# Moving a softmax-row reload one layer earlier in a fused four-layer decode forward and backward, with its zero stores dealt differently

## Chip, cores and metric

The kernel runs on one core of one Trainium2 chip. The metric is the device time of one execution in microseconds (us); lower is better. A core has a matrix engine (PE, with its weight loads shown apart as PEld), a vector engine (DVE), a scalar engine (ACT), GpSimd (POOL) and SyncE (SP), which here only issues transfers; 16 DMA engines carry out the transfers.

## What is computed

One token goes through four layers (attention A, MLP B, A, B, all with shared weights), each with a layer norm and a residual, and then the gradients of all eight inputs are taken for a given `grad_out`. Cut to what matters:

```python
def A(x, k_cache, v_cache, wq, wo):        # 32 heads, 4 key groups, window of the last 4096 keys
    q = (x @ wq) by heads;  k, v = last 4096 rows of the caches
    p = softmax(q k^T / sqrt(128));  return (p v) @ wo
def B(x, w1, b1, w2):
    h = x @ w1 + b1
    return (h * tanh(softplus(h))) @ w2
x = A_x
x = x + A(layernorm(x)); x = x + B(layernorm(x))
x = x + A(layernorm(x)); x = x + B(layernorm(x))
# outputs: x and d/d(A_x, k_cache, v_cache, wq, wo, w1, b1, w2) of <x, grad_out>
```

D is 1024, F 3584, and the caches hold 4 groups x 32768 keys x 128 in bfloat16. Only the last 4096 keys of each group get a gradient. The other 28672 rows of both cache gradients are zeros, and have to be written: 112 stores of 512 KB, 58.7 MB of the 98.8 MB that the kernel writes.

## The kernel before

The layers are called A1, B2, A3, B4; the forward goes through them in this order and the backward comes back. All weights that fit stay in SBUF: `wq`, `wo`, `K` and `V` are four tiles of 8 MB or 4 MB. w1 and w2 do not fit and are streamed through rings of 512 KB buffers. During the MLPs such a ring lies in `K`'s tile (`rings["rb"]`: six buffers over K's groups 1 to 3 in B2's backward), so that K's groups have to be loaded again for A1's backward. `pump` (L172) issues whatever stands next in one written-down queue of loads as soon as its buffer is released by `rel` (L203). K's groups 1, 2 and 3 are the last three entries of that queue; a group needs two buffers, so a group goes out after every second release in the last steps of B2's backward.

All bulk transfers are issued by SP, in the order of the program. The framework gives them eight semaphores in turn, so a transfer is issued only when the one eight issues before it has landed; one whose buffer is not free yet holds up all behind it.

The zero stores are the filler. `zeros(n)` (L139) issues the next n of the 112 from a zeroed source: `zlo` (1024 wide, read twice), `zt` (2048), or, in the last stage, `z8` (4096, which can take two stores in one transfer of 1 MB if they are neighbours and the first has an even number). Where they are issued is written by hand: lists of counts per step (`[8, 4, 17]` in A3's forward, `ZB4` behind the four blocks of B4, `[5, 1, 5]` in A3's backward, L838 in B2's backward, `zeros(4)` and step 0's `zeros(8)` in A1's backward, and a count per output job).

`misc` is a tile of 3072 columns in three parts: `sB` (0 to 1023), `sA` (1024 to 2047) and `zlo`. A1's forward leaves its softmax rows (128 x 1024 bfloat16, 256 KB) in `sA`, and GpSimd stores them to `p1_d` in DRAM (L544), because `sA` then serves as a weight buffer. A3's forward leaves its rows in `sB`. In a layer's backward (`attn_bwd`, L742) the steps are: a product of the gradient with `wo` into two banks (`big`), column sums of it (`acc`), the scores against V (again `big`), a row sum into `sd` (L773), then L776, which forms the score gradient `ds_t` from `big`, `sd` and the softmax rows `p_t`; then `to_keys` transposes it (L436, into `kp`), `keys_mm` multiplies it with K into `R`, and `dqpair` and a product with `wq` follow. In A1's backward (`last`), `p_t` is `wo[:, 0, :]`, free once the first product has read `wo`: GpSimd loads `p1_d` into it (L751), then runs `wo_dead` (L1023: memsets and copies that spread the rows for the output products, which use `wo`'s space as well).

The output stage writes the weight gradients as outer products. Its jobs begin inside A1's backward, from step 3 on (`out_step`): seven pairs for w2 (two halves each), sixteen for w1 interleaved with sixteen for V's and K's gradients (`kv_step`, which takes the softmax rows of A3 and A1 from `p_l` and their score gradients from `ds_l`), then wo and wq. Every job is products on PE, evictions on DVE and ACT into one of seven staging buffers, and a store.

Of the kernel before, what the change touches and what calls it, by code (L numbers as in the profile page):

```python
# [9 lines left out]
BF16 = mybir.dt.bfloat16  # L10
# [4 lines left out]
P = 128  # L15
# [6 lines left out]
def kernel(  # L22
# [22 lines left out]
    nc = tc.nc  # L45
# [15 lines left out]
    WC = W // NC  # L61
# [4 lines left out]
    dram = ctx.enter_context(tc.tile_pool(name="dram", bufs=1, space=bass.MemoryType.DRAM))  # L66
# [17 lines left out]
    wo = kt([P, HQ, D], BF16, "wo")  # L84
# [14 lines left out]
    k_v = A_k_cache[0, :, Sk - W:, :].rearrange("g (p t) d -> p g t d", p=P)  # L99
    v_v = A_v_cache[0, :, Sk - W:, :].rearrange("g (p t) d -> p g t d", p=P)  # L100
    p1_d = dram.tile([P, WC], BF16, name="p1_d")


    x_row, g_row, b_row = kpf[0:TD, 0:P], kpf[0:TD, P:2 * P], kpf[0:NW2, 2 * P:4 * P]
# [34 lines left out]
    def zeros(n, after=None):  # L139
        while n > 0 and zero_jobs:  # L140
            zf, i = zero_jobs.pop(0)
            k = 1
            if zsrc[1] == 4096 and n > 1 and zero_jobs and zero_jobs[0][1] == i + 1 and i % 2 == 0:
                zero_jobs.pop(0)
                k = 2
            dst = zf[:, i * 2048:(i + k) * 2048]
            if zsrc[1] == 1024:
                d = nc.sync.dma_start(dst.rearrange("p (a b) -> p a b", a=2), zlo[:, None, :].to_broadcast([P, 2, 1024]))
            else:
                d = nc.sync.dma_start(dst, zsrc[0][:, 0:k * 2048])  # L150
            gate(d, after)
            after = None
            n -= k
# [588 lines left out]
    def attn_bwd(g_col, g_bf, l, sv, last, nxt, F_, Z_, step):  # L742
        fill_kind("wo")
        big = two_banks()
        for d in range(TD):
            for n in range(8):
                mm(big[n // 4][32 * (n % 4):32 * (n % 4) + 32, :].rearrange("p (h x) -> p h x", h=4),
                   bc(g_bf[:, d:d + 1]), wo[:, 4 * n:4 * n + 4, d * P:(d + 1) * P], d == 0, d == TD - 1, tile_position=(0, 32 * (n % 4)))
        if last:
            p_t, ds_t = wo[:, 0, :], wo[:, 1, :]  # L750
            nc.gpsimd.dma_start(p_t, p1_d[:])  # L751
            wo_dead()
        else:
            p_t, ds_t = sv["p"], sA
        zeros(Z_[0])
        acc = one_tile("acc", HQ)
        j_cols(big, acc, 8, F_[0], True)
        do32 = wk("do32", HQ)
        nc.vector.tensor_copy(pad[:, :, 0:8], acc[:].rearrange("p (g h) -> p g h", g=G))
        nc.vector.tensor_copy(do32[:], acc[:])  # L760
        pr = jkf[:, 0:P]
        nc.vector.tensor_mul(pr[:].rearrange("p (c h) -> p c h", c=NC), do32[:, None, :].to_broadcast([P, NC, HQ]),
                             sv["o32"][:, None, :].to_broadcast([P, NC, HQ]))
        nc.gpsimd.tensor_copy(dos[:, LI[l], :], do32[:])
        step(0)
        fill(F_[1])
        fill_kind("V")
        big = two_banks()
        scores(big, Vf, False)
        sps = sm_tile(P, 1)  # L770
        mm(sps[:], pr[:], one[:], True, True)
        sd = wk("sd", 1)
        nc.vector.tensor_copy(sd[:], sps[:])  # L773
        zeros(Z_[1])
        for h in range(2):
            nc.vector.scalar_tensor_tensor(out=ds_t[:, h * 512:(h + 1) * 512], in0=big[h][:], scalar=sd[:, 0:1],  # L776
                                           in1=p_t[:, h * 512:(h + 1) * 512], op0=ALU.subtract, op1=ALU.mult)
        sv["p"], sv["ds"] = p_t, ds_t
        step(1)
        fill(F_[2])  # L780
        to_keys(ds_t)
        fill_kind("K")
        qacc = one_tile("acc", HQ)
        step(2)
        keys_mm(K[:], fold, qacc, F_[3])
        if not last:
            rings["rb"] += range(2, 8)
            pump()
        nc.scalar.activation(dqpair[:, LI[l], :], qacc[:], ACT.Copy, scale=scale)
        zeros(Z_[2])  # L790
        step(3)
        fill_kind("wq")
        R = one_tile("R", 512)
        for h in range(HQ):
            for hf in range(2):
                g = 2 * hf + h % 2
                mm(R[32 * g:32 * g + 32, :].rearrange("p (t d) -> p t d", t=4), bc(dqpair[:, LI[l], h:h + 1]),
                   wq[:, 4 * hf:4 * hf + 4, h * P:(h + 1) * P], h < 2, h >= HQ - 2, tile_position=(0, 32 * g))
            if h % 4 == 3 and h < 31:
                step(4)  # L800
        y = d_cols(R, hook=lambda: step(5))
        tt = wk("xx", 2 * TD)
        nc.vector.tensor_copy(tt[:, 0:TD], y[:])
        return ln_bwd(tt, sv, g_col, nxt, hook=lambda: step(6))

    def mlp_B2_bwd(g_col, g_bf, sv, x3):
        bcast_g(g_bf)
        R, dps, ds = w2_pass(apair[:, 0, :], g_bf, {10: 1})
        zeros(3)
        dh = kt([P, TF], FP32, "dh_B2")  # L810
        da_merge(dh[:], dps, ds, sv["dact"][:])
        nc.vector.tensor_copy(hpair[:, 1, :], dh[:])
        y = d_cols(R)
        x4_bf = kt([P, TD], BF16, "x4_bf")
        nc.vector.tensor_add(x4_bf[:], x3[:], y[:])

        NT, NV = 4, 3
        dhb = [kpf, jk[:]]
        for hf in range(2):
            for v in range(2):  # L820
                ncb = 2 if v == 0 else 1
                ps = ptile(FP32, "dhp")
                for i in range(ncb):
                    for tt in range(2):
                        col = hf * NW2 + 2 * (NT + 2 * v + i) + tt
                        mm(ps[:, i * 256 + tt:i * 256 + tt + 255:2], bc(hpair[:, 1, col:col + 1], P), ident_bf[:], i == 0 and tt == 0, True)
                evac(dhb[hf][:, v * 512:v * 512 + ncb * 256], ps[:, 0:ncb * 256], ncb * 256, "DA"[(hf + v) % 2])
        nacc = one_tile("acc", TD)
        nv = wk("nv", 16)
        pend = []  # L830

        def pairs(i, w, ring, sl):
            t, hf = i // 2, i % 2
            for k in range(8):
                fb = hf * NW2 + k
                mm(nacc[:, t:t + 1], w[:, k * P:(k + 1) * P], hpair[:, 1, fb:fb + 1], i == 0 and k == 0, hf == 1 and k == 7)
            rel(ring, sl)
            zeros(i in (11, 12, 13, 14))  # L838

        for i in range(16):  # L840
            w, ring, sl = take(("w1h", i))
            T8([w[:, (k // 2) * 256 + k % 2:(k // 2) * 256 + k % 2 + 255:2] for k in range(8)], w[:, 0:1024], "A")
            ttr(w[:, 1024:1792], dhb[i % 2][:, 0:768], nv[:, i:i + 1])
            if pend:
                pairs(*pend.pop())
            pend.append((i, w, ring, sl))
        pairs(*pend.pop())
        tt = wk("xx", 2 * TD)
        n3 = nv[:].rearrange("p (t h) -> p t h", h=2)
        t3 = wk("t3", TD)  # L850
        nc.vector.tensor_add(t3[:], n3[:, :, 0], n3[:, :, 1])
        nc.vector.tensor_add(tt[:, 0:TD], t3[:], nacc[:])
        sv["dh"] = dh
        return ln_bwd(tt, sv, g_col, "A1"), x4_bf
# [133 lines left out]
    def w1_job(t, hf):  # L988
        st = stage()
        wide_job(row_sp["w1"], t, hf, F, st)  # L990
        nc.sync.dma_start(out_6[t * P:(t + 1) * P, hf * (F // 2):(hf + 1) * (F // 2)], st[:, 0:F // 2])
# [27 lines left out]
    w2_out = out_8.rearrange("(c p t) d -> c p t d", p=P, t=2)  # L1019
# [3 lines left out]
    def wo_dead():  # L1023
# [34 lines left out]
        def add(kind, n, f, z=0):  # L1058
            jobs.append((True, f, z))
            while after:  # L1060
                jobs.append((False, after.pop(0), 0))
            for pre, post in prep.get((kind, n), []):
                got = []
                jobs.append((False, lambda pre=pre, got=got: got.append(pre()), 0))
                after.append(lambda post=post, got=got: post(got[0]))

        for n in range(NW2 // 2):
            add("w2a", n, lambda c=2 * n: pair_half(row_sp["w2"], c, w2_out, w2_lhs, 0))
            add("w2", n, lambda c=2 * n: pair_half(row_sp["w2"], c, w2_out, w2_lhs, 1), (0, 0, 1, 1, 0, 0, 1)[n])
        for n in range(16):  # L1070
            add("w1", n, lambda t=n // 2, hf=n % 2: w1_job(t, hf), n in (0, 2, 7))
            add("kv", n, lambda n=n: kv_step(n))
        for n in range(HQ // 8):
            add("wo", n, lambda c=4 * n: tall_jobs(row_sp["wo"], range(c, c + 4), wo_out, wo_lhs))
# [31 lines left out]
        elif i > 2:  # L1106
            run_jobs(1 if i == 4 else 2)

    ZB4 = [10, 10, 10, 8]
    FT4 = [(0, 0, 0, 0), (6, 2, 2, 2), (6, 2, 2, 2), (8, 3)]  # L1110
    FB4 = [(1, 0), (1, 0), (1, 0), (1, 2)]

    pump()
    x1, sA1 = attn_fwd(x0, "A1", True, sA, [0] * 6, [0] * 4)
    x2, sB2, da4 = mlp_B2_fwd(x1)
    x3, sA3 = attn_fwd(x2, "A3", False, sB, [3, 2, 8, 2, 2, 2], [8, 4, 17])
    tt, sB4 = mlp_B4(x3, da4)
    g3, g3b, _ = ln_bwd(tt, sB4, gcol, "A3", nfill=2)
    g2, g2b, _ = attn_bwd(g3, g3b, "A3", sA3, False, "B2", [4, 3, 5, 2], [5, 1, 5], lambda i: None)
# [42 lines left out]
```

## Time and profile before

| | |
|---|---|
| median of three runs | 442.67 us (439.08 to 443.94) |
| profiled execution | 440.81 us, of which its span is 439.0 us |
| bytes moved | 169.45 MB, 386 GB/s over the span |
| busy: PE, DVE, ACT, POOL | 324.2, 234.0, 219.2, 14.7 us |
| SP's transfer queue, share of the 16 engines | 97.9% |
| mean granted TensorE clock | 0.748 |
| store of the softmax rows to DRAM (L544), issue to landing | 6.3 us |
| load of them from DRAM (L751), issue to landing | 8.8 us |
| zero stores from `misc` (98), median issue to landing | 10.7 us |
| loads of a K group (nine), least, median, most | 8.2, 17.7, 20.9 us |

Times in the profile count from the span's start. A group is named by its line, engine, and what it writes from what it reads; a line can be that of a helper (L237 is every product, L257 every transpose of a full tile, L228 and L230 the copies out of PSUM on DVE and ACT, L885 and L888 those of the output stage). In lists of waits the columns are the total, how often, and the longest, in us. A rough map by start of the stage: A1's forward 0, B2's forward 70, A3's forward 114, B4 forward and backward 147, A3's backward 218, B2's backward 249, A1's backward 299, output jobs alone from about 349 on.

### The profile page before, as it was taken

How to read it: one execution, taken by the hardware profiler on the slowest of the kernel's cores; microseconds unless marked ns; L12 is line 12 of the kernel's file. 1: busy time of each engine (PE TensorE's matmuls, PEld its weight loads, DVE VectorE, ACT ScalarE, POOL GpSimd, SP SyncE). 2: the span in 40 equal slices, each digit the busy share in tenths (PEclk: the TensorE clock that was granted, in tenths of full speed). 3: DMA queues.
4: the chain of work that ended last, by engine and by line, in shares of the span. 5: the costliest groups of instructions: out<-in, count | busy, mean ns of one | idle time of the engine just before them, and what ended most of it. 6: DMA issues, size and time to landing. Idle time of an engine off the chain costs nothing.

```text
span 439.0 us, 9214 instructions
## 1 busy us (share of the span) xinstructions
PE 324.2 (74%) x3732; PEld 190.4 (43%) x3732; DVE 234.0 (53%) x532; ACT 219.2 (50%) x335; POOL 14.7 (3%) x52
## 2 busy tenths in 40 slices
PE   3486646378788868778799787897489899999830
PEld 1164215355466656566567465673222322322100
DVE  2035102078345453555546477682146999899950
ACT  1045000047255363555535166682248789899950
POOL 2000000000000000000000000001200020000000
PEclk9998655569699998999999888856765555555555
DMA  8999999999999999899999999999988899999997
GB/s 330 425 421 414 412 408 387 377 368 363 412 411 407 417 403 394 297 385 382 415 403 397 374 408 328 403 329 374 415 345 354 330 392 403 403 406 413 408 414 312
DMA packets 49911, 169.45 MB, mean 386 GB/s; under 512 B 4784, under 2 KB 5836, under 8 KB 45644
## 3 DMA queue, kind: packets, MB, share of 16 engines
q1 hardware_dynamic: 49552, 168.31, 97.9%
q8 instruction: 29, 0.48, 0.4%
q0 software_dynamic: 256, 0.54, 0.3%
q14 instruction: 14, 0.11, 0.1%
q10 hardware_dynamic: 60, 0.01, 0.0%
HBM read 70.00 MB, written 98.84 MB: 385 GB/s over the span
## 4 chain that ended last, share of the span: by engine, by line
PE 22%; DMA 15%; ACT 8%; DVE 4%; issue 2%; ACTq 0%; SPq 0%; DVEq 0%; POOLq 0%
DMA K<-in_B_w_dram 6%; PE R L237 5%; DMA out_dram<-misc 5%; PE tp L257 4%; PE op L237 4%; ACT wo L888 4%; ACT wq L888 3%; PE sm L237 2%; PE acc L237 2%; DMA wo<-p_d 2%; PE lo L237 1%; PE tp L919 1%; DVE wo L885 1%; PE hi L237 1%; DMA out_dram<-wo 1%
## 5 line engine op out<-in xcount | busy, mean ns | idle before, releaser
L230 ACT COPY K<-tp 128x1024 bf16<-128x1024 bf16 x59 | 58.1, 1015 | 17.6 <-PE tp L257 16.5
L257 PE MATMUL tp<-ident_bf,K 128*128 128x128 bf16 x656 | 54.2, 243 | 6.7 <-ACT K L230 3.0
L237 PE MATMUL op<-wo 2*128 2x512 bf16 (+2 forms) x123 | 50.4, 565 | 4.4 <-ACT wo L888 2.2
L257 PEld LDWEIGHTS <-K 128*128 128x128 bf16 x656 | 45.5, 110 | 14.0 <-issue 10.6
L230 ACT COPY wo<-tp 128x1024 bf16<-128x1024 bf16 x33 | 33.5, 1023 | 33.4 <-PE tp L257 30.3
L237 PEld LDWEIGHTS <-wo 128*128 128x128 bf16 (+2 forms) x590 | 23.1, 102 | 55.4 <-issue 45.3
L888 ACT CAST wo<-op 128x512 bf16<-128x512 f32 (+1 forms) x51 | 31.7, 638 | 5.7 <-ACT K L888 1.5
L589 DVE CUSTOM_DVE_ANT_0 K<-K,kp 128x1024 bf16<-128x1024 bf16 (+1 forms) x22 | 24.6, 1127 | 7.2 <-PE R L237 3.8
L228 DVE COPY jk<-R 128x512 f32<-128x512 f32 (+1 forms) x11 | 7.3, 666 | 34.9 <-PE R L237 34.9
L257 PE MATMUL tp<-ident_bf,wo 128*128 128x128 bf16 x336 | 25.7, 231 | 0.3 <-ACT wo L230 0.3
L237 PE MATMUL acc<-wo 2*128 2x512 bf16 (+1 forms) x41 | 24.4, 595 | 0.0
L237 PE MATMUL lo<-wo 2*128 2x512 bf16 x41 | 24.3, 593 | 0.0
L237 PE MATMUL hi<-wo 2*128 2x512 bf16 x41 | 24.3, 592 | 0.0
L257 PEld LDWEIGHTS <-wo 128*128 128x128 bf16 x336 | 20.8, 103 | 7.2 <-issue 7.2
L228 DVE COPY wo<-tp 128x1024 bf16<-128x1024 bf16 x19 | 12.9, 690 | 16.8 <-PE tp L257 16.8
L230 ACT CAST jk<-hi 128x512 bf16<-128x512 f32 x4 | 2.6, 658 | 38.1 <-PE hi L237 38.1
L237 PE MATMUL sm<-wo 2*128 2x512 bf16 (+1 forms) x33 | 20.1, 608 | 0.9 <-DVE cols L377 0.9
L228 DVE COPY K<-tp 128x1024 bf16<-128x1024 bf16 x23 | 15.6, 690 | 9.1 <-PE tp L257 9.0
L885 DVE CAST wo<-op 128x512 bf16<-128x512 f32 (+1 forms) x32 | 18.5, 601 | 3.4 <-PE lo L237 1.7
L228 DVE CAST jk<-lo 128x512 bf16<-128x512 f32 x4 | 2.8, 712 | 32.4 <-PE lo L237 32.4
L237 PE MATMUL R<-wo 2*128 2x512 bf16 (+1 forms) x33 | 19.7, 596 | 0.0
L230 ACT COPY wq<-tp 128x1024 bf16<-128x1024 bf16 x14 | 14.1, 1014 | 11.2 <-PE tp L257 8.4
(293 smaller groups left out, 647.4 us busy)
## 6 DMA issues: line engine op xcount, KB each, us to landing
out_dram<-misc SPq DMA_DIRECT2D x98, 512.0 KB, 10.7
out_dram<-wo SPq DMA_DIRECT2D x36, 512.0 KB, 5.6
K<-in_B_w_dram SPq DMA_DIRECT2D x28, 512.0 KB, 6.8
K<-in_A_k_cache_dram SPq DMA_DIRECT2D x9, 1024.0 KB, 17.7
wq<-in_A_wq_dram SPq DMA_DIRECT2D x8, 1024.0 KB, 10.1
out_dram<-wq SPq DMA_DIRECT2D x8, 1024.0 KB, 11.3
K<-in_B_w_dram SPq DMA_DIRECT2D x16, 448.0 KB, 5.0
out_dram<-wo SPq DMA_DIRECT2D x16, 448.0 KB, 5.8
```

The lines of the kernel that those rows point to most:

```text
L228: return nc.vector.tensor_copy(out_ap, in_ap)
L230: return nc.scalar.copy(out_ap, in_ap)
L237: return nc.tensor.matmul(out_ap, lhsT=lhsT, rhs=rhs, start=start, stop=stop, skip_group_check=True, **kw)
L257: nc.tensor.transpose(ps[:, b * P:(b + 1) * P], ap, ident_bf[:])
L589: return nc.vector.tensor_tensor_reduce(out=w, in0=w, in1=vec, scale=1.0, scalar=0.0, op0=ALU.mult, op1=ALU.add, accum_out=acc_col)
L885: nc.vector.tensor_copy(out_ap, in_ap)
L888: nc.scalar.copy(out_ap, in_ap)
L919: nc.tensor.transpose(ps[:, j * P:(j + 1) * P], spread_t[:, j, :], ident_bf[:])
```

## The change

A1's rows are read back from DRAM in A3's backward, right behind the step that has last read A3's own rows in `sB`: GpSimd first stores A3's rows to a new DRAM buffer `p3_d`, then loads A1's into `sB`. In A1's backward `p_t` is then `sB`, and `wo[:, 0, :]` takes A3's rows from `p3_d`, behind `wo_dead`, for use by V's gradient jobs. In `kv_step` the two layers' rows are thereby found in each other's former place.

The zero stores are counted differently: 14 instead of 17 in A3's last step; 11 instead of 10 behind each of B4's first two blocks; in B2's backward two behind step 9 and one each behind steps 12 and 14, instead of one each behind 11 to 14; one behind each of w2's seven pairs instead of three in all, and none behind w1's jobs instead of three. On SP's queue the end of B2's backward reads, before: K, 2 stores, K, 2 stores, K, 4 stores; after: 2 stores, K, store, K, store, K, 4 stores.

```diff
     p1_d = dram.tile([P, WC], BF16, name="p1_d")
+    p3_d = dram.tile([P, WC], BF16, name="p3_d")
...
         if last:
-            p_t, ds_t = wo[:, 0, :], wo[:, 1, :]
-            nc.gpsimd.dma_start(p_t, p1_d[:])
+            p_t, ds_t = sB, wo[:, 1, :]
             wo_dead()
+            nc.gpsimd.dma_start(wo[:, 0, :], p3_d[:])
         else:
             p_t, ds_t = sv["p"], sA
...
         sv["p"], sv["ds"] = p_t, ds_t
+        if not last:
+            nc.gpsimd.dma_start(p3_d[:], sB)
+            nc.gpsimd.dma_start(sB, p1_d[:])
+            sv["p"] = wo[:, 0, :]
         step(1)
...
             rel(ring, sl)
-            zeros(i in (11, 12, 13, 14))
+            zeros({9: 2, 12: 1, 14: 1}.get(i, 0))
...
-            add("w2", n, lambda c=2 * n: pair_half(row_sp["w2"], c, w2_out, w2_lhs, 1), (0, 0, 1, 1, 0, 0, 1)[n])
+            add("w2", n, lambda c=2 * n: pair_half(row_sp["w2"], c, w2_out, w2_lhs, 1), 1)
         for n in range(16):
-            add("w1", n, lambda t=n // 2, hf=n % 2: w1_job(t, hf), n in (0, 2, 7))
+            add("w1", n, lambda t=n // 2, hf=n % 2: w1_job(t, hf))
...
-    ZB4 = [10, 10, 10, 8]
+    ZB4 = [11, 11, 10, 8]
...
-    x3, sA3 = attn_fwd(x2, "A3", False, sB, [3, 2, 8, 2, 2, 2], [8, 4, 17])
+    x3, sA3 = attn_fwd(x2, "A3", False, sB, [3, 2, 8, 2, 2, 2], [8, 4, 14])
```

## The prediction

> **What bounds the kernel now.** I read the slices first, then the stages, the chain of waits, the timeline around its long wait, and SyncE's own waits. The page's slices show the transfer engines (DMA row) full nearly everywhere and no compute engine full before slice 25. The stages, each asked for by itself, show how full that is in bytes; columns are length, busy us of PE, PEld, DVE, ACT and POOL, granted clock, share of the DMA engines, GB/s:
>
> ```profile
> 292.00:300.00 8.00, 5.67 (x72) 4.62 (x70) 4.78 (x16) 4.53 (x5) 0.00 (x0) 0.50 0.91 285
> 300.00:324.00 24.00, 15.79 (x178) 7.70 (x178) 4.86 (x12) 6.14 (x8) 5.38 (x20) 0.78 1.02 416
> 324.00:352.00 28.00, 25.49 (x169) 7.65 (x168) 22.13 (x48) 21.77 (x41) 0.00 (x0) 0.50 0.82 329
> 352.00:424.00 72.00, 64.81 (x332) 17.54 (x330) 66.90 (x122) 66.92 (x135) 4.42 (x17) 0.50 1.02 405
> 424.00:436.00 12.00, 0.00 (x0) 0.00 (x0) 0.00 (x0) 0.00 (x0) 0.00 (x0) 0.50 1.01 414
> ```
>
> The reader should see two things. After 424 nothing computes and the queue still drains for 12 us, so the end belongs to the transfers: it is the bytes left, at the 405 to 414 GB/s of the last two rows (I use 408), plus whatever holes come before. And there are two holes late in the kernel: 292 to 300 at 285 GB/s lacks (408-285) x 8 = 0.98 MB, or 2.4 us, and 324 to 352 lacks (408-329) x 28 = 2.2 MB, or 5.4 us. Between them lies the wait that the change removes. The chain of waits (start, us, what):
>
> ```profile
> 304.92 0.25 PE lo L237 x4
> 305.18 0.50 issue
> 305.69 8.79 DMA wo<-p_d
> 314.58 1.42 DVE wo L776 x2
> 316.04 0.61 PE tp L436 x4
> 316.65 0.85 PE tp L919 x8
> 317.50 3.39 PE R L237 x27
> ```
>
> In the last attention backward the softmax rows of layer 1 come from DRAM into `wo[:,0,:]`, and L776 waits for them. What else L776 needs was there long before, by the timeline:
>
> ```profile
> 309.00 0.16 DVE L773 COPY cols<-sm 128x1 f32<-128x1 f32 x1 [1.89 <-PE sm L237]
> ...
> 314.58 0.75 DVE L776 SCALAR_TENSOR_TENSOR wo<-lo,cols,wo 128x512 bf16<-128x512 f32 x1 [5.42 <-DMA wo<-p_d]
> ```
>
> That is 5.42 us of pure wait. What is late next is K. Its three head groups reload at 293.0, 295.5 and 299.1, and the product at 317.5 (R from K) reads all of them. No row shows the third one's landing, but SyncE does: each of its transfers waits for the one eight issues before it, and the last of the four 1 MB zero stores that follow (issued 314.69) stands eight behind the third K load:
>
> ```profile
> SPq L150 <- DMA K<-in_A_k_cache_dram: 4.1, 2, 2.1
> ```
>
> The landings of the K loads here are 11.7 to 15.5 us; 299.13 + 15.5 = 314.6 fits that issue at 314.69. So K's last group lands as late as the rows whose load is removed, and the wait is only partly free.
>
> **The parts.** The sum is made on the profiled execution: span 439.0, 440.81 with what lies around it. The runs shown have their median at 442.67, 1.86 above.
>
> *The wait itself.* With the rows already in `sB`, L776 starts at 309.2 instead of 314.58. From its start to the product at 317.44 it now takes 2.86 us (transposes L436, two copies into `kp`, the transposes L919), so the product could start at 309.2 + 2.9 = 312.1, 5.3 us earlier.
>
> *K next.* From 293.0 to 314.6 the engines moved some 7.9 MB (two-microsecond stages added up). The three K loads, the eight 512 KB stores among and behind them and the 256 KB row load are 3.15 + 4.19 + 0.26 = 7.6 MB. So K's last group landed about when everything issued before 305.7 had: transfers share the engines rather than go strictly in turn. After the change four stores still stand ahead of that load and four behind, but two of the eight go out at about 291 (after the step of weight piece 9) instead of 293.8 and 297.7. The hole of 292 to 300 is there because little had been issued; these 1.05 MB go into it. I take 0.8 of its 0.98 MB as filled, 2.0 us, and the third K group at 312.6. The product then starts at 312.7: 4.7 us earlier. Bounds: 5.3 if K is no longer late, and 0.6 if it lands 17.7 us after issue, the median of all nine K loads. By turn alone K's last group would have only 5.24 MB to wait for, and the stages reach that sum at about 308.
>
> The Trainium skill, "DMA: Bandwidth & Descriptors", section "Queues, rings and completion order", says that each transfer engine consumes one queue's descriptors in ring order. By it the chain gains the whole 5.3 us. The trace here disagrees: 308 by ring order, 314.6 by the row.
>
> *The output stage.* Its jobs stand right behind the product, so its first store goes out at about 325.1 - 4.7 = 320.4. What was issued earlier has drained at about 324 today, and at 322 with the first hole filled, so the engines no longer run dry between the two stages. Then w2's seven pairs bring two 512 KB outputs each every (349 - 325)/7 = 3.4 us; with a zero store behind every pair that is 1.57 MB per 3.4 us, 462 GB/s, more than the 408 they can move. Before, only three pairs had one. Four more stores are 2.10 MB against the 2.2 MB of the hole, and I take 4.2 of its 5.4 us as filled: start and the dip at the layer norm remain. Bounds: 2.1 (half) and 5.4. The three stores that left w1's jobs leave a stage at 405 GB/s that is refilled by the backlog. PE, DVE and ACT have the same instructions in the same order; only which tensor holds whose rows is exchanged.
>
> *The count of stores.* 112 in all, as before, but one more of them falls behind 288 (three fewer in layer 3's forward, one more behind each of the first two blocks of layer 4): 512 KB / 408 = +1.3 us.
>
> *What is added early.* Both new steps are on GpSimd's queue behind `dos` at 226.0 and ahead of the memsets at 306.3; the row of POOL shows it idle for 79 us there, so its wait for the store to land and for L776 holds nobody. They move 0.52 MB in a stretch that is full (401 to 408 GB/s at 226 to 240): 1.3 us, set off by the store that is missing ahead of it. The rows stored take some 6.3 us (the same store in layer 1), the ones read back some 8.8: in `sB` by about 242, with 67 us of cover. Without that cover the old wait would be back. The 11th stores of the first two blocks fill a hole at 180 to 184 (141 GB/s) and part of one at 202 to 206, but can hold up the w1 and w2 loads behind them; the three missing ones clear the way for the w1 loads of 159.2, for which PE waited 3.9 us. Taken at 0, bounds -1.5 and +2.6 (1.05 MB in front of the w2 loads, wholly on the path).
>
> *The reload of layer 3's rows.* Same 256 KB as the load removed, issued about 3 us later behind four small GpSimd copies, needed by the first V job at 352: 8.8 us under 40 of cover. `dos` stands behind its 0.6 us issue, and nobody needs that before the w2 jobs are half done. The memsets and spreads ahead of it start 0.6 us earlier. The eight stores of step 0 become five issues (one of 512 KB, three of 1 MB, one of 512 KB), because 97 stores and no longer 98 are gone: one issue on SyncE, behind a full queue.
>
> *Sum on the transfers' side:* -2.0 - 4.2 + 1.3 + 0 = -4.9 us, 440.8 to **435.9**; on the median of the runs 442.67 x 435.9/440.81 = **437.7**. The chain's 4.7 us is not added to this: it is what lets the holes fill.
>
> **Rivals.** *K takes the place of the wait, and nothing early is filled:* the two stores at 291 run beside the last w1 pieces, K's last group lands at 314.6 as now, the chain gains 2.8 us, and only the output stage's hole fills: -4.2 + 1.3 = -2.9, or 437.9 (439.8 on the runs). For it: the third group's lateness in the trace. Against: the hole at 294 to 298.
>
> *All holes fill:* K comes by turn at about 308, the chain gains 5.3, and both holes close: -2.6 (all of the 1.05 MB) - 5.4 + 1.3 = -6.7, 434.1 (436.0). For it: the demand of 462 GB/s. Against: the sum of bytes at K's landing.
>
> *Slower:* layer 2's backward runs on a ring of six weight buffers, and its chain waits for a landing once a round: 6.4, 5.4, 5.2 and 4.8 us. If the extra bytes ahead of the first round (0.52 of rows, 0.52 of the 11th store) and the two stores beside the last raise these two to the 10.7 us median of a zero store, that is +4.3 + 5.9 = +10.2, and the sum +5.3: 446.1 (448.0). It decides from 4.9 us on. For it: the chain passes through just these loads. Against: the first round already runs behind five stores and costs only 1 us more than the others.
>
> **Numbers.** Forecast 0.50, K 0.20, all holes 0.18, slower 0.12. Runs of this kernel spread over 1.1%, so 1% (438.2) is about what can be told. Of the forecast's own range, 434.5 to 440, 0.35 lies below 438.2; with the second rival 0.53 faster, 0.15 + 0.20 = 0.35 the same, 0.12 slower. The range runs from the largest fill with a gain early on (-6.7 - 1.5 on the profiled execution, 432.6) to K's case with the early bound against it, which ends at about no change, 444; only the slower rival is left out.
>
> **What would show it.** Right: L776 directly behind L773; no wait for `p_d`; the R product at about 312 to 313 with a wait for K of under 1 us; 292 to 300 near 390 GB/s; the w2 stage near 400; the last chain step still a drain of 12 us or so. Wrong: K landing at 315 or later; w2 landings in layer 2's backward above 8 us; DVE or ACT waiting for staging buffers in the w2 stage; PE at work until the end.

## The result, and the profile after

The changed kernel takes 439.34 us (median of 20 runs, 436.45 upwards), the kernel before 442.67 us beside it (20 runs): a ratio of 0.9929, with a 95% interval of 0.9900 to 0.9957. By the ratio that is 3.1 us less (1.9 to 4.4), where 4.9 were forecast, and lies inside the 1% called no change. Runs over 1.5% above the fastest of their kernel, one of 477.65 us among them, are not compared. The profiled execution of the kernel after took 439.71 us with a span of 437.9; one profile is one draw from a spread of about 2 us to each side, and between these two the spans differ by 1.1 us only. Line numbers have moved: the softmax step is now L777, its row sum L774, products L238.

The stages of the kernel after, in the columns of before (length, busy us of PE, PEld, DVE, ACT and POOL, granted clock, share of the DMA engines, GB/s):

```profile
292.00:300.00 8.00, 6.48 (x88) 5.51 (x88) 5.90 (x13) 5.22 (x6) 0.00 (x0) 0.57 0.97 340
300.00:324.00 24.00, 18.67 (x224) 8.38 (x228) 8.64 (x23) 10.02 (x16) 5.14 (x20) 0.84 1.03 407
324.00:352.00 28.00, 24.67 (x160) 7.93 (x159) 21.76 (x51) 20.25 (x38) 1.53 (x3) 0.50 1.02 418
352.00:424.00 72.00, 63.27 (x318) 16.43 (x315) 64.99 (x115) 65.79 (x133) 2.72 (x15) 0.50 1.02 409
424.00:436.00 12.00, 0.00 (x0) 0.00 (x0) 0.00 (x0) 0.00 (x0) 0.00 (x0) 0.50 0.76 310
```

The hole of 324 to 352 is gone (329 GB/s before, 418 now), the one of 292 to 300 is half filled (285 to 340). The last row is new: the stage that drained at 414 GB/s now averages 310.

The wait for `p_d` is gone. In the chain of waits (start, us, what) the softmax step follows its row sum, and the product with K follows after the transposes:

```profile
313.33 0.33 PE sm L238 x2
...
313.68 0.17 DVE cols L774
313.85 0.03 issue
313.87 1.42 DVE wo L777 x2
315.29 0.05 issue
315.34 0.40 PE tp L437 x4
315.74 0.45 PE tp L924 x8
316.18 1.87 PE R L238 x32
```

What was not forecast is the first number: the row sum is there at 313.7, not at 309.0, so 4.7 of the 5.42 us won are used up before. The same view shows where, in the first round of w2 loads of layer 2's backward. Before, then after:

```profile
255.62 6.38 DMA K<-in_B_w_dram
```

```profile
251.76 10.24 DMA K<-in_B_w_dram
```

Each row runs from the issue of one w2 load to its landing; both land at 262.0, but the second is the load of the seventh piece, the first that of the eighth. What PE waits for the seventh piece, before and after, is in the timeline:

```profile
260.76 0.40 PE L237 MATMUL R<-K,apair 128*32 128x512 bf16 x4 [1.60 <-DMA K<-in_B_w_dram]
```

```profile
262.05 0.62 PE L238 MATMUL R<-K,apair 128*32 128x512 bf16 x4 [6.28 <-DMA K<-in_B_w_dram]
```

The layer begins 2.7 us earlier than before (245.2, before 247.9) and is 1.3 us late here. The layer norm gradient that ends the layer comes 3.7 us later than before (301.8, before 298.1).

The end, by stretches of 1 us (columns as above), before and after:

```profile
435.00:436.00 1.00, 0.00 (x0) 0.00 (x0) 0.00 (x0) 0.00 (x0) 0.00 (x0) 0.50 1.00 418
436.00:437.00 1.00, 0.00 (x0) 0.00 (x0) 0.00 (x0) 0.00 (x0) 0.00 (x0) 0.50 0.26 107
437.00:438.00 1.00, 0.00 (x0) 0.00 (x0) 0.00 (x0) 0.00 (x0) 0.00 (x0) 0.50 0.02 8
```

```profile
424.00:432.00 8.00, 0.00 (x0) 0.00 (x0) 0.00 (x0) 0.00 (x0) 0.00 (x0) 0.50 1.03 418
432.00:433.00 1.00, 0.00 (x0) 0.00 (x0) 0.00 (x0) 0.00 (x0) 0.00 (x0) 0.50 0.63 262
433.00:434.00 1.00, 0.00 (x0) 0.00 (x0) 0.00 (x0) 0.00 (x0) 0.00 (x0) 0.50 0.14 57
434.00:435.00 1.00, 0.00 (x0) 0.00 (x0) 0.00 (x0) 0.00 (x0) 0.00 (x0) 0.50 0.06 25
435.00:436.00 1.00, 0.00 (x0) 0.00 (x0) 0.00 (x0) 0.00 (x0) 0.00 (x0) 0.50 0.06 25
436.00:437.00 1.00, 0.00 (x0) 0.00 (x0) 0.00 (x0) 0.00 (x0) 0.00 (x0) 0.50 0.02 8
```

A share of 0.06 is one engine of sixteen: by 434 fifteen have finished, and one works on alone to 436.4. Each transfer reports its landing in sixteen parts, and the trace has the time of each: of the last transfer the fifteenth part lands at 434.15, the sixteenth at 436.85. This distance between the last two parts, 2.70 us, is called the gap below. At the end of the kernel before it is 0.33.

**The lead.** Since the end belongs to the transfers, all that follows is read from one quantity: the bytes that a kernel's transfers have moved up to a time T, minus those that the kernel before had moved by then, divided by 0.408 MB per us. A lead that grows in a stretch says that holes of before are filled there. For the profiled executions (a lead in us; the last two columns are how much earlier the last packet ends than the 437.4 of before, and what is missing of it: lead at 424, less the added bytes over 0.408, less that gain):

```
                        profiled  lead at 180  215   280   300   324   352   424 | end  missing
after                    439.71       -2.0    -1.4  -2.5  -1.5  -2.1   4.0   4.7 | 1.0   2.4
stores only              440.13       -2.5     0.8  -1.4  -0.8  -0.8   2.3   0.6 | 0.5   0.1
rows only                437.69        0.3     0.9   1.5  -0.1  -0.3   5.2   5.6 | 3.1   1.2
no row traffic           437.60       -3.5    -1.8  -1.4  -1.1  -1.0   5.0   4.9 | 3.1   2.4
output stores back       439.78       -2.6     0.1  -1.8  -1.0  -1.1   3.9   4.2 | 1.0   1.9
rows later               439.90       -3.9    -4.3  -3.7  -2.3  -2.4   3.7   4.4 | 0.8   2.3
step 9 back              438.03       -1.6     0.1  -0.7  -0.8  -0.9   5.2   4.9 | 2.7   0.9
early deal back          436.31       -1.0     0.7   0.0   1.6   1.6   7.7   8.1 | 4.4   2.4
last store split         443.76       -5.5    -2.7  -4.1  -2.9  -3.6   0.7  -1.6 |-2.9   0.0
rows + step 9            435.80        0.1     2.7   1.0   2.1   2.0   6.9   7.4 | 5.0   1.1
rows + output stores     442.71       -0.9    -1.1  -1.9  -2.7  -3.6   2.5   1.6 |-2.0   2.3
w2 cleared               438.28       -1.6    -0.1  -1.6  -0.3  -0.2   5.9   6.2 | 2.4   2.5
```

For the kernel after: 2.5 us are lost up to 280, 1.0 won from 280 to 300, 0.6 lost up to 324, 6.1 won up to 352 and 0.7 up to 424, which makes the lead of 4.7. Of it 1.3 go into the 0.53 MB added, and 2.4 are missing at the end. What is left is the 1.0 us of this pair of profiles.

What is missing goes with the gap at the end: in eleven of the twelve kernels it is the gap less the 0.33 us of before, within 0.15 us ("step 9 back" has 0.9 for 0.5). And a caution: a profile is one execution. Those of "rows only" and "rows + step 9" are the fastest of their twelve runs, 3.3 and 3.7 us under the median, and that of "last store split" is the slowest, 2.8 above; groups of kernels say more than single rows.

### The profile page after: what moved, and what is told of

Same layout as the page of the kernel before. It is cut to its first block, busy times and chain, and to the rows that moved or that the text cites. A ratio compares the mean times of both kernels' runs of the same rounds, so it can differ in the third digit from the quotient of the medians.

```text
span 437.9 us, 9216 instructions
## 1 busy us (share of the span) xinstructions
PE 322.9 (74%) x3732; PEld 189.0 (43%) x3732; DVE 234.0 (53%) x532; ACT 219.2 (50%) x335; POOL 15.4 (4%) x54
## 4 chain that ended last, share of the span: by engine, by line
PE 18%; DMA 17%; ACT 8%; DVE 4%; issue 2%; SPq 1%; ACTq 0%; DVEq 0%
DMA out_dram<-misc 8%; DMA K<-in_B_w_dram 7%; PE op L238 4%; ACT wo L893 4%; PE R L238 3%; ACT wq L893 2%; PE acc L238 2%; DMA out_dram<-wo 2%; PE sm L238 2%; PE tp L258 2%; ACT K L231 2%; PE lo L238 2%; PE hi L238 1%; PE tp L924 1%; DVE wo L890 1%
## 5 line engine op out<-in xcount | busy, mean ns | idle before, releaser
L258 PE MATMUL tp<-ident_bf,K 128*128 128x128 bf16 x656 | 52.7, 239 | 8.4 <-ACT K L231 3.4
L238 PE MATMUL op<-wo 2*128 2x512 bf16 (+2 forms) x123 | 52.0, 559 | 5.0 <-ACT wo L893 2.7
L258 PEld LDWEIGHTS <-K 128*128 128x128 bf16 x656 | 44.3, 108 | 16.0 <-issue 11.4
L238 PEld LDWEIGHTS <-wo 128*128 128x128 bf16 (+2 forms) x590 | 24.3, 101 | 62.2 <-issue 53.3
L238 PE MATMUL acc<-wo 2*128 2x512 bf16 (+1 forms) x41 | 24.1, 588 | 0.2 <-DVE V L890 0.2
L238 PE MATMUL lo<-wo 2*128 2x512 bf16 x41 | 24.1, 588 | 0.0
L238 PE MATMUL hi<-wo 2*128 2x512 bf16 x41 | 24.0, 586 | 0.0
L238 PE MATMUL sm<-wo 2*128 2x512 bf16 (+1 forms) x33 | 19.8, 600 | 1.3 <-DVE cols L378 1.3
L238 PE MATMUL R<-wo 2*128 2x512 bf16 (+1 forms) x33 | 19.6, 593 | 0.6 <-DVE wo L890 0.4
```

The costliest lines, as they stand in the source:

```text
L238: return nc.tensor.matmul(out_ap, lhsT=lhsT, rhs=rhs, start=start, stop=stop, skip_group_check=True, **kw)
L258: nc.tensor.transpose(ps[:, b * P:(b + 1) * P], ap, ident_bf[:])
```

## The experiments

The theory was: the end is set by the bytes and the holes; the early rows let the output stage start early, and the new deal fills what is left. Rivals: the stores do it without the rows; K takes the wait's place; the early traffic costs in the weight loads what the end gains.

**Only the stores, only the rows.** The first is the kernel before with the counts of after; the second is the kernel after with all counts of before:

```diff
-            zeros({9: 2, 12: 1, 14: 1}.get(i, 0))
+            zeros(i in (11, 12, 13, 14))
...
-    ZB4 = [11, 11, 10, 8]
+    ZB4 = [10, 10, 10, 8]
...
-    x3, sA3 = attn_fwd(x2, "A3", False, sB, [3, 2, 8, 2, 2, 2], [8, 4, 14])
+    x3, sA3 = attn_fwd(x2, "A3", False, sB, [3, 2, 8, 2, 2, 2], [8, 4, 17])
```

(and the counts of the w2 and w1 jobs likewise.)

> The kernel before with the changed deal of the zero stores alone; layer 1's rows are still loaded in its own backward. The changed kernel as a whole stands at 0.993 of the time before. If the deal is what pays (holes of 292 to 300 and 324 to 352 filled), the wait for the rows stays in the chain (some 5 us behind the row sum), and yet the output stage of 324 to 352 moves 400 GB/s or more and the ratio is 0.990 to 0.994. If the two parts are needed together, the stage runs dry at its start as before and the ratio is 0.996 to 1.000.

> The rows' move alone, with the zero stores dealt as before. If the chain is what pays, the wait for the rows is gone, the first output store goes out 3 to 5 us earlier and the ratio is 0.990 to 0.995. If the end belongs to the transfers, the holes of the output stage stay (some 330 GB/s there), half a megabyte more has to be moved, and the ratio is 0.997 to 1.003.

Measured: only the stores 0.9943 (0.9910 to 0.9976), only the rows 0.9989 (0.9960 to 1.0018). The stores alone keep the wait, here 4.26 us (timeline: start, us, engine, line, operation, tiles, and what ended the idle time before):

```profile
311.52 0.16 DVE L773 COPY cols<-sm 128x1 f32<-128x1 f32 x1 [1.89 <-PE sm L237]
315.94 0.75 DVE L776 SCALAR_TENSOR_TENSOR wo<-lo,cols,wo 128x512 bf16<-128x512 f32 x1 [4.26 <-DMA wo<-p_d]
```

The rows alone lose it, and show what becomes of K, whose loads stand in the old order there (the third goes out at 299.45):

```profile
309.94 0.16 DVE L774 COPY cols<-sm 128x1 f32<-128x1 f32 x1 [1.89 <-PE sm L238]
310.14 0.75 DVE L777 SCALAR_TENSOR_TENSOR wo<-lo,cols,misc 128x512 bf16<-128x512 f32 x1
...
312.38 1.91 PE L238 MATMUL R<-K,kp 128*32 128x512 bf16 x32
```

The product starts 2.24 us after the softmax step and waits for nothing: all of K is in by 312.38, 12.9 us after its last issue at the latest. By its landing parts it was in at 311.91, 0.47 us ahead of the product. K does not take the wait's place, not even without the two stores behind step 9, but it is close. The stages of the same two kernels, stores first:

```profile
324.00:352.00 28.00, 25.72 (x169) 7.68 (x168) 22.11 (x48) 21.95 (x42) 0.00 (x0) 0.50 0.95 376
```

```profile
292.00:300.00 8.00, 6.03 (x100) 4.89 (x97) 5.51 (x16) 5.88 (x6) 0.00 (x0) 0.84 0.88 282
324.00:352.00 28.00, 23.17 (x145) 7.38 (x142) 21.00 (x50) 19.17 (x38) 3.00 (x11) 0.50 1.01 408
```

So the hole of the output stage is filled to 408 GB/s by the earlier start alone, with only three stores behind the w2 pairs; with seven stores and the wait it stays at 376. The times do not say the same as the stages: the stores alone are 2.5 us faster than before, the rows alone 0.5, and neither expectation came whole (400 GB/s with this ratio for the stores; a hole that stays for the rows). The intervals of both runs overlap, so their times do not rank rows and stores.

**No traffic of the rows.** The three row transfers are taken out, so that layer 1's score gradient and V's gradient are computed from whatever lies there:

```diff
-            nc.gpsimd.dma_start(wo[:, 0, :], p3_d[:])
...
-            nc.gpsimd.dma_start(p3_d[:], sB)
-            nc.gpsimd.dma_start(sB, p1_d[:])
```

> The changed kernel without its three new row transfers: layer 3's rows are not stored, neither layer's rows are read back, so layer 1's score gradient and V's gradient use other numbers. If the 0.52 MB ahead of the w2 loads of layer 2's backward cost what they weigh (1.3 us) and pass down the chain, the first round of those loads lands in under 9 us (10.2 in the changed kernel's profile) and the ratio goes from 0.993 to 0.989 to 0.991. If they hide, as the prediction took them, the ratio stays at 0.992 to 0.994.

0.9878 (0.9837 to 0.9918), 436.52 us: 2.3 us less than the kernel after, with intervals that just overlap. The transfers left out are 0.79 MB, 1.9 us at 408. In the table of leads its stretches differ from those of the kernel after by up to 1.5 us either way, and the time fits a cost of the rows by their bytes alone. The first w2 loads still land 9.34 us after issue, so it is not the rows that hold these up.

**The rows later.** The store and the reload in B2's backward, behind step 6 of the w2 pass, instead of in A3's:

```diff
+            if c == Z_.get("rows"):
+                nc.gpsimd.dma_start(p3_d[:], sB)
+                nc.gpsimd.dma_start(sB, p1_d[:])
...
-            nc.gpsimd.dma_start(p3_d[:], sB)
-            nc.gpsimd.dma_start(sB, p1_d[:])
...
-        R, dps, ds = w2_pass(apair[:, 0, :], g_bf, {10: 1})
+        R, dps, ds = w2_pass(apair[:, 0, :], g_bf, {10: 1, "rows": 6})
```

> The changed kernel with the two row transfers moved from layer 3's backward (226 to 242, where the engines are full) into layer 2's backward behind its seventh w2 step (about 264 to 276, where they move 244 to 320 GB/s). Leaving all three row transfers out gave 0.988 against 0.993. If that is the weight of the two early ones ahead of the w2 loads, this gives 0.988 to 0.990. If it is the bytes wherever they are, or the third one (the reload at 312), it stays at 0.992 to 0.994.

0.9930 (0.9897 to 0.9964): as the kernel after. Where the bytes stand makes no difference that these runs can tell.

**Each part of the deal put back, or kept alone.** The old counts in the output stage (15 in A3's last step, so that the sum stays 112), the old counts around K, and the old early counts (16 in A3's last step):

```diff
-            add("w2", n, lambda c=2 * n: pair_half(row_sp["w2"], c, w2_out, w2_lhs, 1), 1)
+            add("w2", n, lambda c=2 * n: pair_half(row_sp["w2"], c, w2_out, w2_lhs, 1), (0, 0, 1, 1, 0, 0, 1)[n])
...
-            add("w1", n, lambda t=n // 2, hf=n % 2: w1_job(t, hf))
+            add("w1", n, lambda t=n // 2, hf=n % 2: w1_job(t, hf), n in (0, 2, 7))
```

> The changed kernel with the output stage's stores as before (three among w2's pairs, three among w1's jobs) and the one left over back in layer 3's forward (15 there). If filling the hole of 324 to 352 is worth the 4.2 us of the prediction, the ratio goes to 1.000 to 1.003, and the output stage falls back to some 330 to 360 GB/s. If one transfer engine falls behind the others whenever the queue never runs dry, part of that is not lost: the last transfer's sixteen parts end closer together (2.7 us between the last two in the changed kernel, under 1 us here) and the ratio is 0.994 to 0.998.

```diff
-            zeros({9: 2, 12: 1, 14: 1}.get(i, 0))
+            zeros(i in (11, 12, 13, 14))
```

> The changed kernel with the stores at the end of layer 2's backward one behind each of steps 11 to 14, as before, instead of two behind 9. The prediction has it as a fill of 2.0 us (hole of 292 to 300) and K's last group 2 us earlier: the ratio goes from 0.993 to 0.997. If K is no longer what is late and the end has slack for it, the ratio stays at 0.992 to 0.994.

```diff
-    ZB4 = [11, 11, 10, 8]
+    ZB4 = [10, 10, 10, 8]
...
-    x3, sA3 = attn_fwd(x2, "A3", False, sB, [3, 2, 8, 2, 2, 2], [8, 4, 14])
+    x3, sA3 = attn_fwd(x2, "A3", False, sB, [3, 2, 8, 2, 2, 2], [8, 4, 16])
```

> The changed kernel with layer 3's forward at 16 stores and layer 4's first two blocks at 10, instead of 14 and 11: the same number by the end of layer 4. The prediction took this part at 0, so 0.992 to 0.994. Moving the rows without any new deal gave 0.999, and the whole change without its output stores 0.994; if the early deal is what makes the difference, the ratio goes to 0.997 to 0.999 here.

And the rows with one part each, the early counts as before (17 and 16 in A3's last step):

> The rows' move with only the two stores behind step 9 of layer 2's backward of the new deal; early stores and output stores as before. The rows alone gave 0.999, with any two parts of the deal 0.990 to 0.994. If the stores at the end of layer 2's backward are what fills (the prediction's 2.0 us), 0.992 to 0.995. If stores are worth nothing by place and the difference between those runs is spread, it lies with the rows alone at 0.996 to 1.000.

> The rows' move with only the output stage's stores of the new deal. If they fill that stage's hole, as the prediction had it (4.2 us less 1.3 for the store that comes late), the ratio is 0.990 to 0.994. If the rows' move alone fills it (408 GB/s at 324 to 352 in the profile of the rows alone), these stores are worth nothing and it is 0.996 to 1.000, with 400 GB/s or more in that stage either way.

Measured, in this order: 0.9938 (0.9906 to 0.9970), 0.9932 (0.9902 to 0.9961), 0.9898 (0.9864 to 0.9932), 0.9952 (0.9922 to 0.9982), 0.9946 (0.9909 to 0.9983). All overlap each other: no part of the deal has a time of its own that these runs can tell, and that the early deal costs something (0.9929 against 0.9898) is likely at most. The 0.9898 lies below both cases of its expectation; with the old output counts the output stage still moves 402 GB/s, where 330 to 360 had been expected, and the gap at the end is 2.16 us, not under 1. The leads separate the parts better, because the kernels fall into groups:

- From 280 to 300, nine kernels with two stores behind step 9 gain 1.0 us on average (0.3 to 1.6), the three without lose 0.8 (1.6 to 0.1). The two stores are worth 1.9 us there; 2.0 had been forecast.
- From 324 to 352, kernels with neither wait nor old output counts gain 6.0 to 6.1 (4.3 with the split stores below), those without the wait but with old counts 4.9 to 5.5, the one with the wait and new counts 3.1. The missing wait is worth some 5 us, the stores about 1 once it is gone; but 3.1 are filled by the stores with the wait in place, so both fill the same hole, and which comes first in the count is a choice.
- At 180, the lead goes with the count in A3's last step: 17 stores 0.1 to 0.3, 16 stores -0.9 to -1.6, 15 or 14 stores -1.6 to -5.5. By 280 the seven kernels with 14 or 15 stores there and 11 in layer 4's first blocks stand at -2.2 on average (-0.7 to -4.1), the five others at -0.2 (1.5 to -1.9). The two counts change together in these groups, but the stretch tells them apart: from 146 to 160 alone the seven lose 1.1 to 2.8, 1.8 on average, the five at most 0.3.

That stretch in the kernel after itself, before and after:

```profile
146.00:160.00 14.00, 11.07 (x172) 9.15 (x170) 7.70 (x30) 8.02 (x11) 0.00 (x0) 1.00 1.02 416
```

```profile
146.00:160.00 14.00, 11.14 (x178) 9.29 (x179) 8.51 (x31) 7.74 (x11) 0.00 (x0) 1.00 0.94 367
```

PE's wait for the w1 loads did fall, from 3.9 us to 2.1 (longest 1.3). But the three missing stores left the queue without work: (416 - 367) x 14 / 408 = 1.7 us.

**Stores moved past the first w2 loads**, on top of the old early counts:

```diff
-        R, dps, ds = w2_pass(apair[:, 0, :], g_bf, {10: 1})
+        R, dps, ds = w2_pass(apair[:, 0, :], g_bf, {6: 1, 8: 1, 10: 1, 12: 1})
...
-    g2, g2b, _ = attn_bwd(g3, g3b, "A3", sA3, False, "B2", [4, 3, 5, 2], [5, 1, 5], lambda i: None)
+    g2, g2b, _ = attn_bwd(g3, g3b, "A3", sA3, False, "B2", [4, 3, 5, 2], [5, 1, 2], lambda i: None)
```

> The kernel after with layer 4's counts and layer 3's forward put back as in the run that put back the early deal (10, 10, 10, 8, and 16 in layer 3's last step), and with three of the five zero stores behind the last step of layer 3's backward moved behind steps 6, 8 and 12 of the w2 pass in layer 2's backward, so that 1.57 MB less stands on SyncE's queue ahead of the first round of w2 loads. Theory (what layer 1's rows cost by their early move is paid by layer 2's backward, whose first w2 loads land in 10.2 us instead of 6.4 because more is queued ahead of them): the first round's wait falls to 6 us or less, layer 1's backward begins some 3 us earlier than 301.8 and the ratio to the kernel before is 0.985 to 0.988 (436.2 us or so), below the 0.990 of the run that put back the early deal alone. Rival 1 (the bytes are the limit from here on, and the wait only changes its place: the stores moved now stand in front of the second and third rounds): wait moved, beginning of layer 1's backward within 1 us, ratio 0.989 to 0.992. Rival 2 (the queue runs dry between the two backwards, as at 292 to 300 before): a hole at 245 to 255, ratio 0.993 or more.

0.9888 (0.9846 to 0.9931), 437.08 us from six runs: not to be told from 0.9898. The chain of waits, and the stage of 252 to 262:

```profile
256.44 4.78 DMA K<-in_B_w_dram
...
262.46 8.03 DMA K<-in_B_w_dram
```

```profile
252.00:262.00 10.00, 9.83 (x152) 7.01 (x148) 8.80 (x17) 7.83 (x8) 0.00 (x0) 0.84 0.80 263
```

The first landing shortens as the theory says (7.52 us with the old early counts alone), the second grows as the first rival says, and a hole like the second rival's opens (263 GB/s; 410 with the old early counts alone): 3.6 us of transfer time, (408 - 263) x 10 / 408. The layer norm gradient comes at 300.3, where it came at 298.7 with the old early counts alone. So the theory that the long landings are paid at the end finds no support: the first one went, and nothing was gained. As the hole came with it, what a long landing costs by itself is not shown.

**The tail.** Two tries at why one engine ends late. In the first, twenty one-element GpSimd memsets behind each output job, to see whether more instruction loads delay it more; in the second, the last four single stores are split in 120 and 8 partitions, so that the late engine gets less.

```diff
+            if job:
+                for _ in range(20):
+                    nc.gpsimd.memset(nop_t[0:1, :], 0.0)
```

> The changed kernel with 20 tiny GpSimd memsets behind each output job, some 1300 instructions on an engine that is idle there. In the changed kernel's profile one of the sixteen transfer engines ends 2.7 us behind the other fifteen; the gap opens from 0.1 us at 322 in steps near the instruction loads (329, 355, 375; 16 KB and about 0.95 us each, every one a single packet, so on one engine). If instruction loads make the gap, about 80 KB more of them bring the last part to 4 us or more behind the fifteenth, or a second part falls behind by 2 us or more. If that engine is slow by itself, the gap stays at 2.5 to 2.9 us.

One run, of 515.7 us. The group of the memsets (busy us, mean ns, idle before) and the stage of 352 to 400 tell why:

```profile
L1092 POOL MEMSET nop_t<- 1x1 f32 x1320 | 117.8, 89 | 75.5
```

```profile
352.00:400.00 48.00, 20.18 (x115) 4.61 (x110) 22.56 (x50) 20.15 (x42) 29.70 (x318) 0.50 0.46 180
```

GpSimd, which also spreads the rows for the jobs, became the limit and the queue ran dry. The gap at the end is 0.14 us instead of 2.70, which fits a late engine that catches up when the queue is empty. The question of the instruction loads stays open.

```diff
+            elif zsrc[1] == 4096 and k == 1 and len(zero_jobs) < 4:
+                d = nc.sync.dma_start(dst[0:120], zsrc[0][0:120, 0:2048])
+                nc.sync.dma_start(dst[120:128], zsrc[0][120:128, 0:2048])
```

> The changed kernel with the last four zero stores of the output stage each split into one of 120 rows and one of 8. If rows go to the transfer engines in sixteenths, the last engine is spared 4 x 32 KB, some 5 us of its own time at 1/16 of 410 GB/s, and the first ones get little more. The last part of the changed kernel's last transfer ends 2.7 us behind the fifteenth. If the last engine is the late one, that gap falls under 1 us and the ratio goes from 0.993 to 0.987 to 0.989. If one of the first eight is late, the gap grows to 3 us or more; if another, it stays at 2.6 to 2.8 and the ratio at 0.992 to 0.995.

0.9975 (0.9942 to 1.0008), no better than the kernel after (the intervals overlap), though the tail closes (gap 0.32 us, "missing" 0.0 in the table). That the split closes it is not shown: when the last of the split stores has landed, at 361.7, the gap is still 1.15, and it falls to 0.01 by 421 without any more of them. And more is lost before the end:

```profile
352.00:424.00 72.00, 63.66 (x325) 16.45 (x318) 64.16 (x115) 64.28 (x132) 3.73 (x17) 0.50 1.00 392
```

392 GB/s for 409. The loss lies where the split stores go out: 372 GB/s from 336 to 352 and 324 from 352 to 364, where the kernel after moves 419 and 413. Small transfers that take places among SyncE's eight would explain it, but that was not tried by itself; and this profile, the slowest of its runs, stood 3.6 us behind by 324 already.

## Why the prediction came out as it did

Right in direction, high by 1.8 us in size; the time lies in the range, and the case that came, within 1%, had a chance of 0.35 against 0.53 for faster. That the wait goes and the holes fill came as forecast; how much each part brings did not, and the errors partly cancel. The nearest number, 439.8, is that of the rival in which K takes the wait's place, and that mechanism did not come: luck. Of the signs named, the w2 stage reached 418 GB/s (near 400 forecast), but 292 to 300 only 340 (390), and one sign of being wrong came too: a w2 landing above 8 us (10.24).

- *The wait.* L777 stands directly behind L774, and no wait for `p_d` is left: as forecast. Its time was not: 313.9, forecast 309.2.
- *K next.* Forecast: K's last group at 312.6, the product 4.7 us earlier. By its landing parts K's last group is in at 313.0 (314.67 before), so this term was right to 0.4 us, and it would have held the product for 0.9 us had the chain come at 309.2. K was never waited for in any kernel without the wait, the earliest product being that of 312.38. The product came 1.33 us earlier (316.11 for 317.44) because the layer before it ended late, not for K. The rival in which K takes the place of the wait falls.
- *Step 9's stores,* -2.0: 1.9 by comparison of the groups, 1.0 against the kernel before itself.
- *The output stage,* -4.2: the stage gained 6.1, and for another reason than given. The step "Four more stores ... I take 4.2 of its 5.4 us as filled" credits the stores; by the stages the earlier start alone fills about 5 and the stores then add 1, while the stores alone, with the wait, fill 3.1.
- *Count and bytes,* +1.3: right as a sum: 0.53 MB more are moved in all, 1.3 us.
- *"Taken at 0, bounds -1.5 and +2.6"*, what is added early: this is the term that was mis-sized. In the profiled pair the kernel after stands 2.5 us behind at 280, just within the bound, and the group of kernels with its early counts 2.0 behind the others. It is not the rows, and only to a small part, if at all, the 11th stores ahead of w2: of the 2.0 us some 1.7 arise from 146 to 160, where the three stores fewer in A3's last step, said to clear the way, opened a hole of 1.7 us.
- *The end,* "the bytes left, at the 405 to 414 GB/s": sixteen engines taken as one pool. Of what the kernel is ahead at 424, 2.4 us are missing at the end, because one engine ends late; in the twelve kernels of the table what is missing follows the gap. No term and no rival had this.
- *Slower.* Its mechanism came in part: the first w2 round took 10.2 us instead of 6.4, and layer 2's backward 56.6 instead of 50.3. Its price did not: layer 1's row sum came 4.7 us later than forecast, and the output stage filled all the same. The last round, which was to go to 10.7 as well, stayed at 5.9.

With the terms as the profiled pair has them: -1.0 - 6.1 - 0.1 (300 to 324 and 352 on) + 2.5 + 1.3 + 2.4 = -1.0. Between pairs of profiles this moves by some us, as the table shows; the runs say -3.1.

The reading that transfers share the engines rather than go strictly in turn was wrong. The parts show that in the kernel before the transfers issued from 285 on land in the order of their issue: the store ahead of K's third group is in at 309.85, the group itself at 314.67, the store behind it at 315.77. The Trainium skill's rule of ring order ("DMA: Bandwidth & Descriptors", "Queues, rings and completion order") thus agrees with the trace, and it is the 308 drawn from it that was off. The sum of 5.24 MB leaves out the loads issued before 293.0, which land until 295.3; fifteen parts of the group are in at 312.43, and the sixteenth is 2.2 us late. The awaited rows have such a late part as well, their fifteenth in at 312.64 and their sixteenth at 314.48: of the 5.42 us of wait 1.8 were spent on it.

What stays open: which part of the change pays, rows or stores or which of the stores, within intervals of 0.3%; whether the early deal costs the 1.4 us that 0.9898 suggests; why one engine ends late. The two fastest versions, with the old early counts, are at 0.9898 and 0.9888, below the kernel after but with intervals that reach its own.

## What to carry to other kernels

Where the end is a drain of transfers, account in bytes moved by a given time: a wait that goes is worth the hole that it kept open, while a shorter landing, bought with a hole, brought nothing. A filler transfer taken out of a full stretch to clear the way for a load has a price there too: look at whether the queue then runs dry. When a queue is made free of holes, look at the single engines at its end, not only at their sum.

## What the runs showed of the hardware that was not expected

The sixteen transfer engines do not end together, and the last one can cost as much as a hole. In the kernel after, the last part of a transfer lands 0.09 us behind the fifteenth at 322, 1.13 at 351, 1.94 at 366 and 2.4 at 376; from there on the gap stays between 1.6 and 2.8, and it is 2.70 at the end. In kernels whose queue has holes late, the gap at the end is 0.33 (before), 0.56 (stores only) or 0.14 (the memsets).

But a full queue does not always widen it: with step 9's stores put back the gap falls from 1.78 us at 335 to 0.05 at 375, while the stages from 324 to 352 and from there to 376 move 417 and 398 GB/s. So no engine is shown to be slower throughout, nor that it is always the same one. The kernel before has the gap earlier, 2.2 us at 314, where K's third group lands.

The Trainium skill, "DMA: Bandwidth & Descriptors", "Latency and other measured facts", says that two of the engines are usually slower, and guesses at the descriptor rings of the software queue as the cause. The trace agrees only that an engine can end late; here it is one at the end, nearly all the bytes (168.3 of 170.0 MB) go over SyncE's hardware queue, and no run shows the cause.
